# Interleaving the first two token tiles, full-row layout matmuls, and output tiles grouped by four in a fused attention and gMLP kernel

## The chip, the cores and the metric

The kernel runs on one core of a Trainium2 chip. The metric is the device time of one execution in microseconds (us). Before the change it is 211.75 us, the median of three runs (211.04 to 211.99).

The core has engines with queues of their own: TensorE (PE for its matmuls, PEld for its weight loads), VectorE (DVE), ScalarE (ACT), GpSimd (POOL) and SyncE (SP). Each works its queue in order and waits on semaphores. SP, ACT and POOL can issue DMA transfers, all of which run on the core's 16 DMA engines.

## The reference

The input x has 2048 tokens of 512 numbers (bf16). Two branches read it, and a gate mixes them:

```python
x = A_x
g = _sigmoid((x * gate_w).sum(-1, keepdims=True))
a = _A_ref(x, A_wqkv, A_w_phi, A_wo)
b = _B_ref(x, B_w_in, B_w_sp, B_b_sp, B_w_out)
return g * a + (1 - g) * b
```

Branch A is linear attention with 32 heads of 16. q and k are taken through a 16x16 matrix per head, and softmax(p) and softmax(-p), joined, are the features of each. The sums over tokens of features times v (kv) and of features (z) give num = phi_q kv and den = phi_q z; num / den goes through wo. Branch B is a gated MLP: z = gelu(x w_in) is cut into z1 and z2 of 688 columns; z2 is normalized per token, mixed over the tokens by w_sp (2048x2048), given a bias per token, multiplied with z1 and taken through w_out.

## The kernel before, in words

Tokens are worked in 16 tiles of 128. The tile framework allocates buffers from pools and sets the semaphores; a buffer that is used again waits for its earlier readers. On PE and ACT the order of the work is the program's own (`manual_schedule`); on the other engines the framework's scheduler orders instructions.

**Front** (lines 100 to 301). Identity, masks and constants are made on VectorE and POOL. SP loads the first token tiles (`xs`), part of the z2 weights (`w_z2`, one load for each 128 of 512 input rows) and later everything else; ACT issues three of the `w_z2` loads and `wphiE`. Tokens must lie transposed (`xT`) to be a matmul's weights. Tiles 0 to 3 are transposed on PE by `x_T` (four transposes, one VectorE copy), the others by DMA. `warm_up` matmuls on constants fill PE at the start (lines 277 to 284). `z2_tile` then multiplies a tile with `w_z2`: eight matmuls of 344 or 345 columns into one two-bank PSUM tile `zp`, then a Gelu on ACT and the statistics on VectorE. The extra column is the gate, put into `w_z2` by `gate_T` (line 237), which turns the loaded gate row by a transpose with 4 active rows. `b_T` (line 243) turns the bias with 16 active rows, and `wphi_fold` (line 248) spreads the 16x16 matrices with 16 active rows. Tile 0 and tile 1 follow one another, and `gate_T`, `x_T(1)`, `x_T(2)` and `x_T(3)` are put between their matmuls.

**k and v** (lines 496 to 519). For each tile: `k_tile` (four matmuls, two Exp, row sums, evening out on VectorE and POOL), `v_tile`, `kv_acc` into `kvacc`, and one half of a mixing tile, `gg_half`: 16 matmuls of 344 columns, one VectorE instruction into `ucat`, and after the second half a DMA transpose into `uT` from SP. Six q tiles (`q_tile`) are put into this stage too. A q tile's features are transposed by DMA into `eqT`.

**Attention and output** (lines 520 to 532). The slot i holds `attn_tile(i)` (eight matmuls of 68 columns into `at`, then `rden` and `o` on VectorE and a DMA transpose into `oT` from SP), `q_tile(i+6)` while there are any, one half of a mixing tile, and on even slots from 2 on `ba_pair`. `ba_pair` computes two output tiles: for each, four matmuls with `oT` and five with `uT` (`ba_main`), then one matmul for the 48 rows left over (`ba_rem`). In a pair these two matmuls have 64 active rows each, one in the upper and one in the lower half of the array. The results go out through ACT (`ba_store`: scale into `ob`, then a DMA issue on ACT's queue). Tiles 14 and 15 come last (`ba_tile`), tile 15 in two halves of 256 columns, the second of which goes through VectorE and SP.

[...] In the last two stages `kvacc`/`at` takes two, and the other six are the buffers of `mm` (`mm_tile`), which q, k, v, mixing and output tiles all take in turn. `ob` has the two buffers that are the default of its pool `work`.

Of the kernel before, what the change touches and what calls it, by code (L numbers as in the profile page):

```python
# [10 lines left out]
FP32 = mybir.dt.float32  # L11
# [3 lines left out]
P = 128  # L15
# [20 lines left out]
def kernel(  # L36
# [33 lines left out]
    z2all = pers.tile([P, NT, FH], BF16, name="z2all")  # L70
    z1all = pers.tile([P, NT, FH], BF16, name="z1all")
    wqkT = early.tile([P, 8, D], BF16, name="wqkT")
    wphiE = early.tile([DH, H, DH], BF16, name="wphiE")
    eexp = early.tile([DH, P], BF16, name="eexp")
    wphi = early.tile([P, NDT, P], BF16, name="wphi")
    mask_bd = early.tile([P, P], BF16, name="mask_bd")
    mask64 = pers.tile([P, NG, DH], BF16, name="mask64")
# [15 lines left out]

    ident = early.tile([P, P], BF16, name="ident")
    xs = early.tile([P, 4, D], BF16, name="xs")
    gaterow = early.tile([NDT, P], BF16, name="gaterow")
    brow = early.tile([NT, P], BF16, name="brow")
    zeros = early.tile([P, 32], BF16, name="zeros")

    w_in_v = B_w_in.rearrange("(dt p) f -> p dt f", p=P)  # L100

    ones32 = early.tile([P, 32], BF16, name="ones32")
    ramp = early.tile([P, 2, 32], BF16, name="ramp")
    nc.vector.memset(zeros[:], 0.0)
    nc.vector.memset(ones32[:], 1.0)
    nc.vector.tensor_tensor_scan(
# [5 lines left out]
    for q in range(4):  # L112
        qs = slice(32 * q, 32 * q + 32)
        nc.vector.tensor_tensor(
            out=ident[qs, qs], in0=ramp[qs, 0, :], in1=ramp[qs, 1, :], op=ALU.is_equal)
    nc.gpsimd.dma_start(out=gaterow[:, :], in_=gate_w.rearrange("(dt p) -> dt p", p=P))
    nc.gpsimd.dma_start(out=brow[:, :], in_=B_b_sp.rearrange("(t p) -> t p", p=P))
    def load_z2w(eng, dt):
        eng.dma_start(out=w_z2[:, dt, 0:FH], in_=w_in_v[:, dt, FH:F])

    nc.sync.dma_start(out=xs[:, 0, :], in_=x2[0:P, :])
    load_z2w(nc.scalar, 0)
    load_z2w(nc.sync, 1)
    load_z2w(nc.scalar, 2)
    nc.sync.dma_start(out=xs[:, 1, :], in_=x2[P:2 * P, :])
    load_z2w(nc.scalar, 3)
    nc.sync.dma_start(
        out=xs[:, 2:4, :], in_=x2[2 * P:4 * P, :].rearrange("(i p) d -> p i d", p=P))
# [7 lines left out]
            out=xT[:, :, q * CH:(q + 1) * CH], in_=x2[q * CH:(q + 1) * CH, :]  # L136
        )
    nc.sync.dma_start_transpose(out=wqkT[:, :, :], in_=A_wqkv[:, 0:2 * D])
    nc.scalar.dma_start(out=wphiE[:, :, :], in_=A_w_phi.rearrange("h e f -> e h f"))
    nc.sync.dma_start(  # L140
        out=wv_sb[:, :, :],
        in_=A_wqkv[:, 2 * D:3 * D].rearrange("(dt p) n -> p dt n", p=P),
# [37 lines left out]
    def z_mm(tt, wt, w, order=None, mid={}):  # L180
        zp = psA.tile([P, 2, CH], FP32, name="zp")
        for dt, j in order or [(dt, j) for dt in range(NDT) for j in range(2)]:
            n = HF if j == 0 else w - HF
            nc.tensor.matmul(  # L184
                zp[:, j, 0:n], lhsT=xT[:, dt, tt * P:(tt + 1) * P],
                rhs=wt[:, dt, j * HF:j * HF + n],
                start=(dt == 0), stop=(dt == NDT - 1),
            )
            for f in mid.get((dt, j), ()):
                f()  # L190
        return zp

    def z2_tile(tt, **kw):
        zp = z_mm(tt, w_z2, FH + 1, **kw)
# [5 lines left out]
        nc.vector.bn_aggr(out=mv[:, tt, :], in_=bn6[:, tt, :, :].rearrange("p j s -> p (j s)"))  # L200

    def z1_tile(tt):
        zp = z_mm(tt, w_z1, FH)
# [15 lines left out]
                op0=ALU.subtract, op1=ALU.mult,  # L219
            )  # L220

    wp = psA.tile([P, 2, CH], FP32, name="zp")

    def warm_up(n, w=CH):
        for _ in range(n):
# [4 lines left out]
    def x_T(i):  # L230
        tp = psF.tile([P, NDT, P], BF16, name="tp", tag="pq", bufs=2)
        for dt in range(NDT):
            nc.tensor.transpose(tp[:, dt, :], xs[:, i, dt * P:(dt + 1) * P], ident[:, :])  # L233
        with tc.high_priority():
            nc.vector.tensor_copy(out=xT[:, :, i * P:(i + 1) * P], in_=tp[:, :, :])  # L235

    def gate_T():
        gt = psF.tile([P, NDT], BF16, name="gt", tag="pq", bufs=2)
        nc.tensor.transpose(gt[:, :], gaterow[:, :], ident[0:NDT, 0:NDT])
        for dt in range(NDT):  # L240
            nc.vector.tensor_copy(out=w_z2[:, dt, FH:FH + 1], in_=gt[:, dt:dt + 1])

    def b_T():
        bt = psF.tile([P, NT], BF16, name="bt", tag="pq", bufs=2)
        nc.tensor.transpose(bt[:, :], brow[:, :], ident[0:NT, 0:NT])
        nc.vector.tensor_copy(out=bT[:, :], in_=bt[:, :])

    def wphi_fold():
# [26 lines left out]

    with tc.manual_schedule(engines={mybir.EngineType.PE, mybir.EngineType.Activation}):
        warm_up(7)
        x_T(0)
        warm_up(5, P)
        z2_tile(  # L280
            0, order=[(0, 0), (1, 0), (2, 0), (0, 1), (1, 1), (2, 1), (3, 0), (3, 1)],
            mid={(2, 0): [gate_T, lambda: x_T(1)], (2, 1): [lambda: warm_up(4, P)]},
        )
        z2_tile(1, mid={(1, 1): [lambda: x_T(2)], (2, 1): [lambda: x_T(3)]})
        z2_tile(2)
        z2_tile(3)
        b_T()
        for c in range(NCH):
            ts = list(range(c * 4, c * 4 + 4))
            for tt in ts:  # L290
                if c > 0:
                    z2_tile(tt)
                if c >= 2 and tt % 2 == 0:
                    fold(3 - c, (tt % 4) // 2)
            for tt in ts:
# [9 lines left out]
    early_cm.__exit__(None, None, None)  # L305
    psM = ctx.enter_context(
        tc.tile_pool(name="psM", bufs=1, space=bass.MemoryType.PSUM, reuse_waits="tile"))
    work = ctx.enter_context(tc.tile_pool(name="work", bufs=2, reuse_waits="tile"))
    kvp_cm = tc.tile_pool(name="kvp", bufs=2, side="right", reuse_waits="tile")
    kvp = kvp_cm.__enter__()  # L310

    def mm_tile():
        return psM.tile([P, CH], FP32, name="mm", tag="mm", bufs=6)

    def expo(pool, name, bufs, tt, w):
        ps = mm_tile()
# [103 lines left out]
    def attn_tile(tt):  # L420
        at = psM.tile([P, 8, P], FP32, name="at", tag="kvat", bufs=1)
        for g in range(8):
            nc.tensor.matmul(  # L423
                at[:, g, 0:AW], lhsT=eqTs[tt][:, g, :], rhs=kvz[:, g, :], start=True, stop=True)
# [12 lines left out]
        oTs[tt] = oT  # L437

    def u_T(tt):
        uT = work.tile([P, NFT, P], BF16, name="uT", bufs=9)  # L440
        nc.sync.dma_start_transpose(out=uT[:, :, :], in_=ucat[tt % NU][:, :])
        return uT

# [19 lines left out]
            nc.scalar.activation(out=ob[:, :], in_=acc, func=AF.Copy, scale=g_inv[:, tt:tt + 1])  # L463
            nc.scalar.dma_start(out=dst, in_=ob[:, :])

    def ba_tile(tt, nsplit=1):
        w = D // nsplit
        for h in range(nsplit):
            acc = mm_tile()
            ba_main(acc[:, 0:w], tt, h * w, (h + 1) * w)  # L470
            ba_rem(acc[:, 0:w], tt, slice(0, P), h * w, (h + 1) * w)
            ba_store(acc[:, 0:w], tt, h * w, (h + 1) * w, h > 0)

    def ba_pair(p):
        accs = [mm_tile() for _ in range(2)]
        for s_ in range(2):
            ba_main(accs[s_][:, :], 2 * p + s_)
        for s_ in range(2):
            ba_rem(accs[s_][:, :], 2 * p + s_, halves[s_])
        for s_ in range(2):  # L480
            ba_store(accs[s_][:, :], 2 * p + s_, 0, D, False)

    oTs = {}
    uTs = {}
    eqTs = {}
    Q_AT = (5, 7, 9, 11, 13, 15)
    ggs = [(tt, j) for tt in range(NT) for j in range(2)]

# [6 lines left out]
    with tc.manual_schedule(engines={mybir.EngineType.PE, mybir.EngineType.Activation}):  # L495
# [36 lines left out]
        ba_tile(15, nsplit=2)  # L532


# [28 lines left out]
```

## Time and profile before

| | |
|---|---|
| median of three runs | 211.75 us (211.04 to 211.99) |
| profiled execution | 211.67 us |
| its span, first to last instruction | 210.0 us |
| granted TensorE clock | 1.000 |
| start of the k stage on PE, by the chain of waits | 46.65 us |
| end of the last mixing tile's matmuls | 201.30 us |

A line of a timeline or of the chain of waits has the start, the length, the engine, the source line, what is written and what is read (buffer numbers left out), and how many instructions are merged. Times on PE are between the starts of pipelined matmuls: the mean length of one in the groups (309 ns for 344 columns) is longer than the 146 ns from one start to the next, and the latter is what each costs. "Idle before <- releaser" says how long the engine stood and what ended it. The `LNNN` in the lines are those of the kernel before.

### The profile page before, as it was taken

What the parts mean: (1) busy time and instruction counts of PE and PEld (TensorE: products, weight loads), DVE (VectorE), ACT (ScalarE), POOL (GpSimd) and SP (SyncE); (2) the same over time, 40 slices, a digit from 0 to 9 for tenths busy, and PEclk for the clock granted to TensorE, in tenths of its full rate; (3) what the DMA queues carried; (4) which work ended last, traced back from release to release, by engine and by line L of the source; (5) the groups of instructions that cost most, each with busy time, mean ns of one, the idle gap of its engine ahead of it and who ended that gap; (6) DMA issues with size and microseconds to landing.
All of it is one profiled execution on the core that took longest, in us unless ns stands there. A gap on an engine that the chain in (4) does not pass through costs nothing.

```text
span 210.0 us, 3753 instructions
## 1 busy us (share of the span) xinstructions
PE 203.5 (97%) x1437; PEld 121.8 (58%) x1456; DVE 131.6 (63%) x284; ACT 73.2 (35%) x119; POOL 46.4 (22%) x77
## 2 busy tenths in 40 slices
PE   8999999999999999999999999999999999999983
PEld 3666666665656565655556666464655555646442
DVE  3576786765996787979779669446554735415120
ACT  2366656668223323232332223150504240202120
POOL 7020202020643242425252223204040402000000
PEclk9999999999999999999999999999999999999999
DMA  6999999999910204214040599895567574435241
GB/s 196 263 164 242 256 274 189 267 274 185 272 37 3 39 4 85 54 36 89 3 87 0 118 333 146 162 128 112 125 92 150 104 134 83 107 64 101 41 112 50
DMA packets 88994, 27.20 MB, mean 130 GB/s; under 512 B 82864, under 2 KB 88976, under 8 KB 88976
## 3 DMA queue, kind: packets, MB, share of 16 engines
q1 hardware_dynamic: 83680, 22.45, 57.0%
q10 hardware_dynamic: 5232, 4.51, 7.0%
q8 instruction: 11, 0.18, 0.4%
q14 instruction: 7, 0.06, 0.1%
q0 software_dynamic: 64, 0.01, 0.0%
HBM read 4.41 MB, written 2.10 MB: 31 GB/s over the span
## 4 chain that ended last, share of the span: by engine, by line
PE 93%; DMA 3%; issue 1%; DVE 1%; SPq 0%
PE mm L410 36%; PE zp L184 18%; PE mm L318 13%; PE mm L449 8%; PE mm L358 7%; PE mm L447 6%; PE at L423 2%; DMA xs<-in_A_x_dram 2%; PE kvacc L374 2%; DMA uT<-ucat 1%; PE mm L452 1%; PE fps L265 1%; PE tp L233 0%; DVE ucat L415 0%; DVE ob L459 0%
## 5 line engine op out<-in xcount | busy, mean ns | idle before, releaser
L410 PE MATMUL mm<-z2all,wspT 128*128 128x344 bf16 x512 | 79.8, 309 | 0.1
L410 PEld LDWEIGHTS <-wspT 128*128 128x128 bf16 x512 | 48.7, 98 | 24.1
L184 PE MATMUL zp<-w_z,xT 128*128 128x344 bf16 (+1 forms) x256 | 39.9, 310 | 0.0
L184 PEld LDWEIGHTS <-xT 128*128 128x128 bf16 x256 | 24.3, 98 | 11.3 <-DVE xT L235 0.2
L322 ACT ACTIVATE eq<-mm 128x512 bf16<-128x512 f32 x32 | 17.4, 594 | 35.9 <-PE mm L318 23.4
L326 DVE TENSOR_REDUCE zs<-eq 128x64 f32<-128x1024 bf16 x16 | 19.4, 1216 | 15.5 <-ACT eq L322 15.5
L463 ACT ACTIVATE ob<-mm,g_inv 128x512 bf16<-128x512 f32 (+1 forms) x16 | 10.8, 674 | 51.6 <-PE mm L452 48.3
L335 POOL TENSOR_TENSOR eq<-eq,ratio 128x512 bf16<-128x512 bf16 x16 | 16.9, 1058 | 45.5 <-DVE ratio L334 24.0
L322 ACT ACTIVATE ek<-mm 128x512 bf16<-128x512 f32 x32 | 17.2, 602 | 25.0 <-PE mm L318 25.0
L415 DVE SCALAR_TENSOR_TENSOR ucat<-mm,bT,z1all 128x344 bf16<-128x344 f32 x32 | 18.0, 563 | 8.3 <-PE mm L410 7.4
L326 DVE TENSOR_REDUCE zs<-ek 128x64 f32<-128x1024 bf16 x16 | 19.2, 1208 | 2.8 <-ACT ek L322 2.8
L449 PE MATMUL mm<-slabs,uT 128*128 128x512 bf16 (+1 forms) x82 | 19.9, 366 | 0.9 <-DMA uT<-ucat 0.8
L426 DVE RECIPROCAL rden<-at 128x32 f32<-128x32 f32 x16 | 5.4, 338 | 22.6 <-PE at L423 22.6
L318 PEld LDWEIGHTS <-xT 128*128 128x128 bf16 x128 | 11.8, 97 | 10.8 <-issue 0.2
L335 POOL TENSOR_TENSOR ek<-ek,ratio 128x512 bf16<-128x512 bf16 x16 | 16.9, 1059 | 2.2 <-DVE ratio L334 1.3
L358 PE MATMUL mm<-wv_sb,xT 128*128 128x512 bf16 x63 | 16.4, 379 | 0.1
L318 PE MATMUL mm<-wk_p,xT 128*128 128x512 bf16 x57 | 15.8, 379 | 0.4
L447 PE MATMUL mm<-slabs,oT 128*128 128x512 bf16 (+1 forms) x65 | 16.0, 366 | 0.2
L318 PE MATMUL mm<-wq_p,xT 128*128 128x512 bf16 x59 | 15.6, 378 | 0.2
L196 ACT ACTIVATE z2all<-zp 128x688 bf16<-128x688 f32 x16 | 11.9, 744 | 10.8 <-PE zp L184 10.8
L199 DVE BATCH_NORM_STATS2 bn<-z2all 128x6 f32<-128x344 bf16 x32 | 14.9, 502 | 0.0
L204 ACT ACTIVATE z1all<-zp 128x688 bf16<-128x688 f32 x16 | 11.9, 744 | 6.9 <-PE zp L184 6.9
(73 smaller groups left out, 151.9 us busy)
## 6 DMA issues: line engine op xcount, KB each, us to landing
out_dram<-ob ACTq DMA_DIRECT2D x15, 128.0 KB, 2.6
slabs<-in_B_w_out_dram ACTq DMA_DIRECT2D x2, 640.0 KB, 6.8
w_z<-in_B_w_in_dram SPq DMA_DIRECT2D x2, 344.0 KB, 4.6
w_z<-in_B_w_in_dram ACTq DMA_DIRECT2D x3, 172.0 KB, 3.5
wv_sb<-in_A_wqkv_dram SPq DMA_DIRECT2D x1, 512.0 KB, 4.5
slabs<-in_A_wo_dram ACTq DMA_DIRECT2D x1, 512.0 KB, 3.6
xs<-in_A_x_dram SPq DMA_DIRECT2D x2, 128.0 KB, 3.6
xs<-in_A_x_dram SPq DMA_DIRECT2D x1, 256.0 KB, 5.0
```

The lines of the kernel that those rows point to most:

```text
L184: nc.tensor.matmul(zp[:, j, 0:n], lhsT=xT[:, dt, tt * P:(tt + 1) * P], rhs=wt[:, dt, j * HF:j * HF + n], start=(dt == 0), stop=(dt == NDT ...
L196: nc.scalar.activation(out=z2v, in_=zp[:, :, 0:HF], func=AF.Gelu_apprx_tanh)
L199: nc.vector.bn_stats(out=bn6[:, tt, j, :], in_=z2v[:, j, :])
L318: nc.tensor.matmul(ps[:, :], lhsT=xT[:, dt, tt * P:(tt + 1) * P], rhs=w[:, dt, :], start=(dt == 0), stop=(dt == NDT - 1))
L322: nc.scalar.activation(out=e[:, :, a, :], in_=ps[:, :].rearrange("p (h f) -> p h f", f=DH), func=AF.Exp, scale=1.0 - 2.0 * a)
L326: nc.vector.tensor_reduce(out=z[:].rearrange("p h a -> p (h a)"), in_=e[:].rearrange("p h a f -> p (h a) f"), axis=AX.X, op=ALU.add,)
L335: nc.gpsimd.tensor_tensor(out=e[:, :, 1, :], in0=e[:, :, 1, :], in1=ratio[:, :, None].to_broadcast([P, H, DH]), op=ALU.mult)
L358: nc.tensor.matmul(v_ps[:, :], lhsT=xT[:, dt, tt * P:(tt + 1) * P], rhs=wv_sb[:, dt, :], start=(dt == 0), stop=(dt == NDT - 1))
L410: nc.tensor.matmul(gp[:, 0:HF], lhsT=wspT[:, st, tt * P:(tt + 1) * P], rhs=z2all[:, st, j * HF:(j + 1) * HF], start=(st == 0), stop=(st == ...
L415: nc.vector.scalar_tensor_tensor(out=ucat[tt % NU][:, c0 + j * HF:c0 + (j + 1) * HF], in0=gp[:, 0:HF], scalar=bT[:, tt:tt + 1], in1=z1all[ ...
L447: nc.tensor.matmul(acc, lhsT=oT[:, g, :], rhs=wo_t[:, g, c0:c1], start=(g == 0), stop=False)
L449: nc.tensor.matmul(acc, lhsT=uT[:, i + ft, :], rhs=w_main[i][:, ft, c0:c1], start=False, stop=False)
```

## The change

- Front: tile 0 and tile 1 have a function of their own, `z2_first_two`, which interleaves their matmuls in a new order with two short warm-ups instead of nine. `x_T(0)` is split: the first 128 columns are copied by VectorE, the other 384 by ACT. The second token tile's load goes ahead of a weight load on SP, and weight loads 1 and 2 swap queues.
- `gate_T`, `b_T` and `wphi_fold` work on 128 rows: their row inputs become 128-row tiles whose other rows are set to zero by memsets on VectorE and POOL. `gate_T` and `b_T` become matmuls with the identity.
- Output: `ba_step` computes one output tile's main part in each slot into one of four accumulators of their own. After the last tile of a group of four (in the end, of two) the left-over rows of the whole group and then its stores follow. The other PSUM tiles of this stage have two buffers.
- `attn_tile` runs one slot ahead, behind the mixing half; slot 0 has two mixing halves, and the last mixing half moves one slot earlier.
- Tile 15 is cut at column 384 instead of 256. `eqT` has 7 buffers instead of 8, `oT` 5 instead of 4, `uT` 11 instead of 9.

```diff
-    wphiE = early.tile([DH, H, DH], BF16, name="wphiE")
-    eexp = early.tile([DH, P], BF16, name="eexp")
+    wphiE = early.tile([P, H, DH], BF16, name="wphiE")
+    eexp = early.tile([P, P], BF16, name="eexp")
-    gaterow = early.tile([NDT, P], BF16, name="gaterow")
-    brow = early.tile([NT, P], BF16, name="brow")
+    gaterow = early.tile([P, P], BF16, name="gaterow")
+    brow = early.tile([P, P], BF16, name="brow")
+    nc.vector.memset(gaterow[:], 0.0)
-    nc.gpsimd.dma_start(out=gaterow[:, :], in_=gate_w.rearrange("(dt p) -> dt p", p=P))
-    nc.gpsimd.dma_start(out=brow[:, :], in_=B_b_sp.rearrange("(t p) -> t p", p=P))
+    nc.gpsimd.dma_start(out=gaterow[0:NDT, :], in_=gate_w.rearrange("(dt p) -> dt p", p=P))
+    nc.gpsimd.memset(brow[:], 0.0)
+    nc.gpsimd.memset(wphiE[:], 0.0)
+    nc.gpsimd.dma_start(out=brow[0:NT, :], in_=B_b_sp.rearrange("(t p) -> t p", p=P))
     nc.sync.dma_start(out=xs[:, 0, :], in_=x2[0:P, :])
     load_z2w(nc.scalar, 0)
-    load_z2w(nc.sync, 1)
-    load_z2w(nc.scalar, 2)
     nc.sync.dma_start(out=xs[:, 1, :], in_=x2[P:2 * P, :])
+    load_z2w(nc.scalar, 1)
+    load_z2w(nc.sync, 2)
     load_z2w(nc.scalar, 3)
-    nc.scalar.dma_start(out=wphiE[:, :, :], in_=A_w_phi.rearrange("h e f -> e h f"))
+    nc.scalar.dma_start(out=wphiE[0:DH, :, :], in_=A_w_phi.rearrange("h e f -> e h f"))
...
+    def z2_first_two():
+        zps = [zp_tile() for _ in range(2)]
+
+        def one(tt, dt, j):
+            z_one(zps[tt], tt, w_z2, FH + 1, dt, j)
+
+        x_T(0, True)
+        warm_up(2, P)
+        one(0, 0, 0)
+        x_T(1)
+        one(0, 1, 0)
+        one(1, 0, 0)
+        one(1, 1, 0)
+        gate_T()
+        one(0, 2, 0)
+        one(1, 2, 0)
+        for dt in range(3):
+            one(0, dt, 1)
+        x_T(2)
+        one(0, 3, 0)
+        one(0, 3, 1)
+        z2_out(0, zps[0])
+        for dt in range(3):
+            one(1, dt, 1)
+        x_T(3)
+        one(1, 3, 0)
+        one(1, 3, 1)
+        z2_out(1, zps[1])
...
+    def x_T(i, split=False):
+        for k, dts in enumerate([range(1), range(1, NDT)] if split else [range(NDT)]):
+            tp = psF.tile([P, NDT, P], BF16, name="tp", tag="pq", bufs=2)
+            for dt in dts:
+                nc.tensor.transpose(tp[:, dt, :], xs[:, i, dt * P:(dt + 1) * P], ident[:, :])
+            d = slice(dts[0], dts[-1] + 1)
+            if k == 1:
+                nc.scalar.copy(out=xT[:, d, i * P:(i + 1) * P], in_=tp[:, d, :])
+            else:
+                with tc.high_priority():
+                    nc.vector.tensor_copy(out=xT[:, d, i * P:(i + 1) * P], in_=tp[:, d, :])
     def gate_T():
-        nc.tensor.transpose(gt[:, :], gaterow[:, :], ident[0:NDT, 0:NDT])
-        for dt in range(NDT):
-            nc.vector.tensor_copy(out=w_z2[:, dt, FH:FH + 1], in_=gt[:, dt:dt + 1])
+        nc.tensor.matmul(gt[:, :], lhsT=gaterow[:, :], rhs=ident[:, 0:NDT], start=True, stop=True)
+        nc.vector.tensor_copy(out=w_z2[:, :, FH], in_=gt[:, :])
     def b_T():
-        nc.tensor.transpose(bt[:, :], brow[:, :], ident[0:NT, 0:NT])
+        nc.tensor.matmul(bt[:, :], lhsT=brow[:, :], rhs=ident[:, 0:NT], start=True, stop=True)
...
     with tc.manual_schedule(engines={mybir.EngineType.PE, mybir.EngineType.Activation}):
         warm_up(7)
-        x_T(0)
-        warm_up(5, P)
-        z2_tile(
-            0, order=[(0, 0), (1, 0), (2, 0), (0, 1), (1, 1), (2, 1), (3, 0), (3, 1)],
-            mid={(2, 0): [gate_T, lambda: x_T(1)], (2, 1): [lambda: warm_up(4, P)]},
-        )
-        z2_tile(1, mid={(1, 1): [lambda: x_T(2)], (2, 1): [lambda: x_T(3)]})
+        z2_first_two()
...
+    psK_cm = tc.tile_pool(name="psK", bufs=6, space=bass.MemoryType.PSUM, reuse_waits="tile")
+    mm_pool = psK_cm.__enter__()
     def mm_tile():
-        return psM.tile([P, CH], FP32, name="mm", tag="mm", bufs=6)
+        return mm_pool.tile([P, CH], FP32, name="mm")
-        eqT = work.tile([P, 8, P], BF16, name="eqT", bufs=8)
+        eqT = work.tile([P, 8, P], BF16, name="eqT", bufs=7)
-        oT = work.tile([P, NG, P], BF16, name="oT", bufs=4)
+        oT = work.tile([P, NG, P], BF16, name="oT", bufs=5)
-        uT = work.tile([P, NFT, P], BF16, name="uT", bufs=9)
+        uT = work.tile([P, NFT, P], BF16, name="uT", bufs=11)
...
+    def acc_tile():
+        return psC.tile([P, CH], FP32, name="acc")
+    def ba_step(tt):
+        group = next(g for g in BA_GROUPS if tt in g)
+        accs[tt] = acc_tile()
+        ba_main(accs[tt][:, :], tt)
+        if tt == group[-1]:
+            for t in group:
+                ba_rem(accs[t][:, :], t, halves[t % 2])
+            for t in group:
+                ba_store(accs[t][:, :], t, 0, D, False)
+    BA_GROUPS = [range(0, 4), range(4, 8), range(8, 12), range(12, 14)]
...
-        for i in range(NT):
-            attn_tile(i)
+        psK_cm.__exit__(None, None, None)
+        mm_pool = ctx.enter_context(
+            tc.tile_pool(name="psG", bufs=2, space=bass.MemoryType.PSUM, reuse_waits="tile"))
+        psC = ctx.enter_context(
+            tc.tile_pool(name="psC", bufs=4, space=bass.MemoryType.PSUM, reuse_waits="tile"))
+        attn_tile(0)
+        for i in range(NT - 1):
             if i + nq < NT:
                 q_tile(i + nq)
-            if ggs:
+            gg_next()
+            attn_tile(i + 1)
+            if i == 0:
                 gg_next()
-            if i >= 2 and i % 2 == 0:
-                ba_pair((i - 2) // 2)
+            elif i < NT - 1:
+                ba_step(i - 1)
         ba_tile(14)
-        ba_tile(15, nsplit=2)
+        ba_tile(15, cuts=(0, 384, D))
```

More of the change, by code (lines that the diff above doesn't have):

```diff
@@ L178, with zp_tile, z_one, z_mm @@
     psA = psA_cm.__enter__()
[L180 to L187, printed above, removed]
-            )
-            for f in mid.get((dt, j), ()):
-                f()
-        return zp
-    def z2_tile(tt, **kw):
-        zp = z_mm(tt, w_z2, FH + 1, **kw)
+    def zp_tile():
+        return psA.tile([P, 2, CH], FP32, name="zp")
+    def z_one(zp, tt, wt, w, dt, j):
+        n = HF if j == 0 else w - HF
+        nc.tensor.matmul(
+            zp[:, j, 0:n], lhsT=xT[:, dt, tt * P:(tt + 1) * P],
+            rhs=wt[:, dt, j * HF:j * HF + n],
+            start=(dt == 0), stop=(dt == NDT - 1),
+        )
+    def z_mm(tt, wt, w):
+        zp = zp_tile()
+        for dt in range(NDT):
+            for j in range(2):
+                z_one(zp, tt, wt, w, dt, j)
+        return zp
+    def z2_out(tt, zp):
         z2v = z2all[:, tt, :].rearrange("p (j n) -> p j n", j=2)
@@ L200, in z2_tile @@
         nc.vector.bn_aggr(out=mv[:, tt, :], in_=bn6[:, tt, :, :].rearrange("p j s -> p (j s)"))
+    def z2_tile(tt):
+        z2_out(tt, z_mm(tt, w_z2, FH + 1))
+    def z2_first_two():
[24 more added lines that the diff above has]
+        z2_out(1, zps[1])
     def z1_tile(tt):
@@ L220, in z2_norm @@
             )
-    wp = psA.tile([P, 2, CH], FP32, name="zp")
+    wp = zp_tile()
     def warm_up(n, w=CH):
@@ L228, in warm_up @@
                 rhs=nc.const_aps.tensor(1.0, [P, w], BF16), start=True, stop=True)
-    def x_T(i):
-        tp = psF.tile([P, NDT, P], BF16, name="tp", tag="pq", bufs=2)
-        for dt in range(NDT):
-            nc.tensor.transpose(tp[:, dt, :], xs[:, i, dt * P:(dt + 1) * P], ident[:, :])
-        with tc.high_priority():
-            nc.vector.tensor_copy(out=xT[:, :, i * P:(i + 1) * P], in_=tp[:, :, :])
+    def x_T(i, split=False):
[9 more added lines that the diff above has]
+                    nc.vector.tensor_copy(out=xT[:, d, i * P:(i + 1) * P], in_=tp[:, d, :])
     def gate_T():
-        gt = psF.tile([P, NDT], BF16, name="gt", tag="pq", bufs=2)
-        nc.tensor.transpose(gt[:, :], gaterow[:, :], ident[0:NDT, 0:NDT])
-        for dt in range(NDT):
-            nc.vector.tensor_copy(out=w_z2[:, dt, FH:FH + 1], in_=gt[:, dt:dt + 1])
+        gt = psF.tile([P, NDT], FP32, name="gt", tag="pq", bufs=2)
+        nc.tensor.matmul(gt[:, :], lhsT=gaterow[:, :], rhs=ident[:, 0:NDT], start=True, stop=True)
+        nc.vector.tensor_copy(out=w_z2[:, :, FH], in_=gt[:, :])
     def b_T():
-        bt = psF.tile([P, NT], BF16, name="bt", tag="pq", bufs=2)
-        nc.tensor.transpose(bt[:, :], brow[:, :], ident[0:NT, 0:NT])
+        bt = psF.tile([P, NT], FP32, name="bt", tag="pq", bufs=2)
+        nc.tensor.matmul(bt[:, :], lhsT=brow[:, :], rhs=ident[:, 0:NT], start=True, stop=True)
         nc.vector.tensor_copy(out=bT[:, :], in_=bt[:, :])
@@ L277 @@
         warm_up(7)
-        x_T(0)
-        warm_up(5, P)
-        z2_tile(
-            0, order=[(0, 0), (1, 0), (2, 0), (0, 1), (1, 1), (2, 1), (3, 0), (3, 1)],
-            mid={(2, 0): [gate_T, lambda: x_T(1)], (2, 1): [lambda: warm_up(4, P)]},
-        )
-        z2_tile(1, mid={(1, 1): [lambda: x_T(2)], (2, 1): [lambda: x_T(3)]})
+        z2_first_two()
         z2_tile(2)
@@ L464, in ba_store, with ba_tile @@
             nc.scalar.dma_start(out=dst, in_=ob[:, :])
[L466 to L481, printed above, removed]
+    def acc_tile():
+        return psC.tile([P, CH], FP32, name="acc")
+    def ba_tile(tt, cuts=(0, D)):
+        for h, (c0, c1) in enumerate(zip(cuts, cuts[1:])):
+            acc = acc_tile()[:, 0:c1 - c0]
+            ba_main(acc, tt, c0, c1)
+            ba_rem(acc, tt, slice(0, P), c0, c1)
+            ba_store(acc, tt, c0, c1, h > 0)
+    def ba_step(tt):
[7 more added lines that the diff above has]
+                ba_store(accs[t][:, :], t, 0, D, False)
     oTs = {}
@@ L485 @@
     eqTs = {}
+    accs = {}
+    BA_GROUPS = [range(0, 4), range(4, 8), range(8, 12), range(12, 14)]
     Q_AT = (5, 7, 9, 11, 13, 15)
```

## The prediction

> **What bounds the kernel now.** I read the page's engine shares first, then PE's waits, then the chain of waits stage by stage, then ScalarE's timeline, because the change rearranges what ScalarE and PE share. The shares:
>
> ```profile
> PE 203.5 (97%) x1437; PEld 121.8 (58%) x1456; DVE 131.6 (63%) x284; ACT 73.2 (35%) x119; POOL 46.4 (22%) x77
> ```
>
> PE is busy through the span and the others are not. What PE waits for, by the waits of PE:
>
> ```profile
> PE zp L226 <- PEq L547: 0.8, 1, 0.8
> PE mm L449 <- DMA uT<-ucat: 0.8, 1, 0.8
> PE tp L233 <- DMA xs<-in_A_x_dram: 0.5, 1, 0.5
> ```
>
> Only 2.1 us. So this change cannot win by removing large waits; it can win at the start, at the end, and in what the "busy" share hides: warm-ups and drains. Everything on PE is on the path, so a microsecond saved or lost there is one of span.
>
> **The front.** The chain of waits from 4 to 13 us (start, length, what):
>
> ```profile
> 1.74 4.41 DMA xs<-in_A_x_dram
> 6.19 0.40 PE tp L233 x4
> ...
> 8.88 2.63 PE zp L184 x18
> 11.51 0.11 PE bt L245
> ```
>
> PE stands until the second token tile lands at 6.15, its load being third on SP's queue (issued 1.74). A matmul of 344 columns takes 2.63/18 = 0.146. Tile 2 starts two matmuls into the x18 piece (PE's timeline puts its first start at 8.71): at 9.01. In the changed order: warm-ups end at 3.79 as now; x_T(0) at 0.107 a transpose (half speed) to 4.22; two warm-ups to 4.43. Now the 512-column VectorE copy starts 0.24 after its last transpose and takes 0.42; the 128-column piece, 0.2 by estimate, ends under the warm-ups. One matmul (0.29 at half speed) to 4.72. xs1 is now second on SP, where w_z2[1] landed at 4.53 with more bytes, so x_T(1) runs to 5.1. Its copy ends at 5.75; two matmuls of tile 1 to 6.05. w_z2[2], third on SP, takes the place that landed at 6.15: 6.2, then five matmuls to 6.93. x_T(2) needs xs2-3, which landed at 7.19 (issued 2.21, 5.0 to land). If that stays, 7.24 + 0.22 + seven matmuls 1.02 + x_T(3) 0.22 = 8.70: gain 0.3. If it lands by 6.93: 8.39, gain 0.6. I take 0.45. For earlier speaks that wphiE (16 KB in small pieces, 5.2 to land in the DMA view) now waits on POOL for its memset (128x512, 0.53 by the slabs memset) and comes later on the same DMA engines. Bounds -0.3 to 0.8: the same memset holds ScalarE's queue at the wphiE issue (2.23 now), with the table load (1.28) and the second part of x_T(0)'s copy (128x384, 0.58 between the 0.475 of 256 and the 0.687 of 512 columns) behind it. That copy then ends near 5.3, and its matmul still comes before 5.75, while PE waits for x_T(1)'s copy. VectorE's gaterow memset (0.11, as ident's) is over long before xs0. If ScalarE were another 0.5 later, the gain would be gone.
>
> [...] The trace shows seven warm-ups of 427 ns and short ones of 107, then 147 ns per 344 columns from 5.15 on. The change drops seven of nine short warm-ups. [...] By the row PE is continuously busy in my layout from 0.85 to 5.25[...]. I take 0.
>
> **128-row layout matmuls.** The chain from 24 to 32:
>
> ```profile
> 25.74 0.32 PE wps L251 x4
> ...
> 27.34 0.22 PE fps L265 x4
> ```
>
> Four 128-column matmuls with 16 rows cost 0.10 more than four with 128; the eight after them take 1.28 instead of 1.17. So 0.2 goes. b_T takes 0.11 plus the entry gap (11.34 to 11.44) and would cost about 0.06 with 128 rows: 0.15. gate_T lay in the xs1 wait: 0. The single copy of its column replaces four of 0.15 on VectorE, off the path. Sum 0.35.
>
> **Left-over rows by fours.** The chain from 129 to 165:
>
> ```profile
> 146.51 0.32 PE mm L452 x2
> 146.83 0.36 PE at L423 x8
> 147.19 0.86 PE mm L318 x4
> 148.06 2.33 PE mm L410 x16
> 150.39 0.26 PE at L423 x8
> ```
>
> Two 64-row matmuls of 512 columns run beside each other in 0.32, 0.10 more than one full matmul (0.86/4 = 0.215); the eight matmuls after them take 0.36 instead of 0.26. So entering and leaving the half-row shape costs 0.20. Seven pairs become three fours and one pair: 3 x 0.20 = 0.6. If four did not overlap as two by two, 0.215 more each, and the gain is nil; the pair is the nearest row, so 0.6.
>
> **The end.** The chain from 196 to 210:
>
> ```profile
> 201.93 2.76 DMA uT<-ucat
> ...
> 204.73 0.72 PE mm L449 x5
> ...
> 206.69 0.48 DVE ob L459
> ```
>
> PE's timeline has the last oT matmul before the wait begin its 0.108 at 203.69; the next starts at 204.73: 0.94 lost. In the changed order the last gg is followed by attn (0.26), ba_step(13) (9 x 0.215 = 1.94), a pair (0.32) and ba_tile(14) (2.15): 4.7 until tile 15 is wanted. uT(15) lands 0.61 + 0.04 + 2.76 = 3.4 after gg. oT(15), issued behind it on SP (1.21), lands at 1.87 + 2.5 = 4.4, or 4.97 with the 3.1 of a lone transpose, bounding its wait at 0.3. I take 0: gain 0.94. The last store is 128 columns, not 256: VectorE 0.48 to about 0.33 (344 columns of ucat take 0.57), 0.15. Together 1.1.
>
> Gains: 0.45 + 0.35 + 0.6 + 1.1 = 2.5.
>
> **What it adds: a burst on ScalarE.** The timeline of ScalarE (ACT) around one pair:
>
> ```profile
> 146.87 0.69 ACT L463 ACTIVATE ob<-mm,g_inv 128x512 bf16<-128x512 f32 x1 [5.40 <-PE mm L452]
> 147.59 0.34 ACTq L464 DMA_DIRECT2D out_dram<-ob  x1
> 148.03 0.69 ACT L463 ACTIVATE ob<-mm,g_inv 128x512 bf16<-128x512 f32 x1 [0.47 <-ACT ob L463]
> 148.74 0.36 ACTq L464 DMA_DIRECT2D out_dram<-ob  x1
> 149.20 1.09 ACT L322 ACTIVATE eq<-mm 128x512 bf16<-128x512 f32 x2 [0.49 <-ACT ob L463]
> ```
>
> A store takes 1.16 of ScalarE, and the next q tile's two Exp queue behind the stores in program order. Now that harms nobody: mm has six buffers. Afterwards four stores stand ahead of the Exp, ob has two buffers, so the third waits for the first to land, and q and gg share two PSUM buffers: q(12) cannot start until q(11)'s Exp are over.
>
> Let q(11) start at 0, just after the four's left-over rows. Store 1 is active from -0.11 (0.36 after its matmul, as above), its DMA leaves at 0.61; store 2's at 1.77. The landing times of single stores in the ob view are 2.0 and 2.2 where a transpose went just before, 1.7 with none, 2.6 behind oT's. At 2.1 store 3 starts at 2.78, store 4 at 3.94 (store 2 has then just landed), the Exp at 5.10, ending 6.19. PE wants the buffer after 0.86 + 2.33 + 0.26 + 1.94 = 5.39. So PE stands 0.86. This happens after tiles 0-3 (q(12)) and 4-7 (the gg after q(15)); after 8-11 no Exp is left. Sum 1.7. Bounds: 0.5 each at 1.7, 1.4 each at 2.6. [...] Here all four go through ScalarE. By the pair's row alone (two stores, 1.16 each) the Exp would end at about 3.3 and nothing would wait[...].
>
> VectorE's queue behind a late Exp: q(11)'s row sums (1.2), then whatever is ordered after them. If the gg's ucat (0.57), ready at 3.2, stood behind, the next gg would wait 0.9 more; I take 0, its order following readiness. The two gg at slot 0 meet VectorE's backlog: 0 to 0.6, taken 0. SP's late eqT is wanted only four slots later. The attention step moves behind gg: its VectorE work and its oT issue on SP now come after ucat and uT, and oT(i+1), 3.1 to land, is wanted two slots (over 9 us) later: 0. POOL's brow load goes behind two memsets (0.7) and is wanted near 11: 0. eqT with seven, oT with five, uT with eleven buffers each free a slot before need: 0. The end's stores have two ob buffers for tiles 12, 13, 14, ready 2.5 apart: 0.
>
> Net: -2.5 + 1.7 = -0.8 against the profiled execution's 211.67 (span 210.0 and 1.67 around it), 210.9; it lies 0.08 under the median of the runs, so I leave it.
>
> **Rivals.** (a) No hold: stores land faster or queue differently, so PE never waits. Then 211.7 - 2.5 = 209.2. For it: 1.7 was seen; against it: two ob buffers and four stores need over 5.39. (b) The front does not change, because xs2-3 and w_z2[2] set it: 211.3 to 211.7 with the hold. That edit then does not do what it says. (c) Slower: out stores land at 4.1 and 3.7, as the ob view has for the first pair (136 to 141), next to two transposes. Store 3 then waits till 4.8, the Exp end at 8.2, PE stands 2.8 twice: 211.7 - 2.5 + 5.6 = 214.8. It turns slower when a hold exceeds 1.25, a landing of about 2.5, and beyond 0.5% at 3.0. Against it: one pair of seven did so.
>
> **How the numbers follow.** A difference under 0.5% (1.06 us) can hardly be told from none. The hold case, 0.60: 209.8 to 211.9, half below 210.7. Case (a), 0.17: 208.9 to 209.7. Case (b), 0.11. Case (c), 0.09 beyond 0.5%; VectorE's order, 0.03, near 211.8. Faster 0.30 + 0.17 = 0.47; same 0.30 + 0.11 + 0.03 = 0.44; slower 0.09. Range 209.2 to 212.2.
>
> **What would show it.** A PE gap of about 0.9 before the matmuls of q(12) and before the gg after q(15), ended by ACT eq; store 3 of each four starting on its DMA's landing; wps at 0.22; left-over rows 0.53 for four; no uT wait at the end; tile 2 at about 8.55. Wrong if PE shows no wait for ACT in the attention slots, or a half-clock stretch after 5.3.

## The result and the profile after

The changed kernel takes 210.24 us (median of four runs, 210.04 to 210.44) against 211.62 us for the kernel before on the same chip. The ratio is 0.9937, with a 95% interval of 0.9912 to 0.9962: 0.6% faster, 1.4 us. The profiled execution took 210.28 us with a span of 208.6, so the two spans differ by 1.39. All line numbers from here on are those of the kernel that a block names.

The waits of PE in the changed kernel (engine, tile, line, releaser: us in total, times, longest):

```profile
PE zp L265 <- PEq L598: 0.8, 1, 0.8
PE mm L449 <- DVE ucat L454: 0.4, 1, 0.4
PE zp L188 <- DMA w_z<-in_B_w_in_dram: 0.3, 1, 0.3
PE zp L188 <- DVE xT L279: 0.2, 1, 0.2
```

The wait for uT is gone. A wait for a weight load and one for VectorE's `ucat` are new. Now the same stages as before the change. The front, by the chain of waits:

```profile
1.76 5.12 DMA w_z<-in_B_w_in_dram
6.88 0.04 issue
6.92 0.89 PE zp L188 x5
...
8.99 2.63 PE zp L188 x18
11.62 0.01 PE bt L288
```

PE no longer stands for the second token tile but for weight load 2, which landed at 6.88. Tile 2 starts two matmuls into the x18 piece; in PE's timeline that is 9.12, against 9.01 before. The bias matmul, 0.11 before, is 0.01. The head matrices, chain from 24 to 32:

```profile
25.66 0.22 PE wps L294 x4
25.88 1.17 PE zp L188 x8
27.05 0.22 PE fps L308 x4
```

The four `wps` matmuls now take what the four `fps` take (0.22, with 0.32 before), and the eight behind them are at 1.17 where they had 1.28. In the attention slots, by the chain from 190 to 209, a four of left-over rows and what follows, then the end:

```profile
190.99 0.54 PE acc L491 x4
191.53 2.44 PE mm L449 x16
...
203.07 0.22 PE acc L491
203.28 0.65 PE acc L486 x4
...
205.51 0.35 DVE ob L498
```

Four left-over rows take 0.54, and the sixteen matmuls after them 2.44 instead of 2.33: one entry and one exit for four tiles. At the end PE runs through, and the last store takes 0.35 on VectorE instead of 0.48.

The predicted burst is there too. The chain from 148 to 157:

```profile
149.20 0.69 ACT ob L502
...
149.91 2.44 DMA out_dram<-ob
...
152.43 0.70 ACT ob L502
...
153.59 0.69 ACT ob L502
...
154.75 1.09 ACT eq L361 x2
155.84 0.04 issue
155.88 1.18 PE mm L449 x7
```

Store 3 starts on the landing of store 1, store 4 follows, the two Exp of q(11) come last. Yet what waits for them is not q(12) but the mixing half behind it (L449), and it waits only 0.31 (0.529 between two starts in PE's timeline where 0.215 is usual). PE's waits above do not list so short a stand. The second burst, whose first store took 4.0 to land, holds nobody: the mixing half after q(15) starts before the Exp of q(15), by the timelines of PE and ScalarE:

```profile
177.24 2.50 PE L449 MATMUL mm<-z2all,wspT 128*128 128x344 bf16 x16
178.82 1.08 ACT L361 ACTIVATE eq<-mm 128x512 bf16<-128x512 f32 x2 [0.47 <-ACT ob L502]
```

The other new wait is in slot 0, chain from 123 to 128:

```profile
122.93 1.18 PE mm L449 x8
124.11 0.03 issue
124.13 0.59 DVE ucat L454
124.72 0.04 issue
124.76 2.49 PE mm L449 x16
```

The second mixing half of slot 0 stands behind VectorE's `ucat` of the first, which begins as soon as that half's matmuls are done: 0.58 between the starts (0.609 less 0.03). Only the eight attention matmuls lie in between.

By stage, from PE's starts in the two profiles: first matmul of tile 4 at 11.55 before and 11.49 after (-0.06); first attention matmul at 120.90 and 120.48 (another -0.35); from there to the last matmul 85.48 and 84.77 (-0.71); from that to the end of the span 3.58 and 3.32 (-0.26).

### The profile page after: what moved, and what is told of

Read it like the earlier page. It is cut to its first block, busy times and chain, and to the rows that moved or that the text cites. A ratio compares the mean times of both kernels' runs of the same rounds, so it can differ in the third digit from the quotient of the medians.

```text
span 208.6 us, 3745 instructions
## 1 busy us (share of the span) xinstructions
PE 202.5 (97%) x1432; PEld 121.5 (58%) x1449; DVE 131.2 (63%) x282; ACT 75.0 (36%) x121; POOL 47.0 (23%) x79
## 4 chain that ended last, share of the span: by engine, by line
PE 91%; DMA 4%; ACT 2%; issue 1%; DVE 0%; SPq 0%; ACTq 0%
PE mm L449 35%; PE zp L188 18%; PE mm L357 12%; PE acc L488 8%; PE mm L397 7%; PE acc L486 6%; DMA w_z<-in_B_w_in_dram 2%; PE kvacc L413 2%; PE at L462 2%; DMA out_dram<-ob 1%; PE acc L491 1%; ACT ob L502 1%; PE fps L308 1%; ACT eq L361 1%; ACTq L503 0%
## 5 line engine op out<-in xcount | busy, mean ns | idle before, releaser
L449 PE MATMUL mm<-z2all,wspT 128*128 128x344 bf16 x512 | 79.9, 309 | 0.6 <-DVE ucat L454 0.4
L449 PEld LDWEIGHTS <-wspT 128*128 128x128 bf16 x512 | 49.0, 98 | 26.3 <-issue 1.4
L188 PEld LDWEIGHTS <-xT 128*128 128x128 bf16 x256 | 24.5, 98 | 12.1 <-DVE xT L279 0.7
L454 DVE SCALAR_TENSOR_TENSOR ucat<-mm,bT,z1all 128x344 bf16<-128x344 f32 x32 | 17.4, 545 | 21.2 <-PE mm L449 21.2
L502 ACT ACTIVATE ob<-acc,g_inv 128x512 bf16<-128x512 f32 (+1 forms) x16 | 10.9, 680 | 33.9 <-PE acc L491 23.2
L488 PE MATMUL acc<-slabs,uT 128*128 128x512 bf16 (+2 forms) x85 | 20.1, 366 | 0.0
L357 PEld LDWEIGHTS <-xT 128*128 128x128 bf16 x128 | 12.3, 98 | 13.0 <-PE acc L491 0.8
L357 PE MATMUL mm<-wq_p,xT 128*128 128x512 bf16 x62 | 16.3, 379 | 0.1
L486 PE MATMUL acc<-slabs,oT 128*128 128x512 bf16 (+2 forms) x61 | 15.6, 365 | 0.4
L488 PEld LDWEIGHTS <-uT 128*128 128x128 bf16 x85 | 8.2, 98 | 9.2
```

The costliest lines, as they stand in the source:

```text
L188: nc.tensor.matmul(zp[:, j, 0:n], lhsT=xT[:, dt, tt * P:(tt + 1) * P], rhs=wt[:, dt, j * HF:j * HF + n], start=(dt == 0), stop=(dt == NDT ...
L357: nc.tensor.matmul(ps[:, :], lhsT=xT[:, dt, tt * P:(tt + 1) * P], rhs=w[:, dt, :], start=(dt == 0), stop=(dt == NDT - 1))
L449: nc.tensor.matmul(gp[:, 0:HF], lhsT=wspT[:, st, tt * P:(tt + 1) * P], rhs=z2all[:, st, j * HF:(j + 1) * HF], start=(st == 0), stop=(st == ...
L454: nc.vector.scalar_tensor_tensor(out=ucat[tt % NU][:, c0 + j * HF:c0 + (j + 1) * HF], in0=gp[:, 0:HF], scalar=bT[:, tt:tt + 1], in1=z1all[ ...
L486: nc.tensor.matmul(acc, lhsT=oT[:, g, :], rhs=wo_t[:, g, c0:c1], start=(g == 0), stop=False)
L488: nc.tensor.matmul(acc, lhsT=uT[:, i + ft, :], rhs=w_main[i][:, ft, c0:c1], start=False, stop=False)
```

## The experiments

Theory: the gains of the prediction came about except at the front. The hold did not, because the two PSUM buffers of q and mixing tiles are not taken in turn, as the prediction's sum needed. In the program as built q(12) has the buffer of the mixing half before it, not q(11)'s, and the half after q(15) has the other one, not q(15)'s. Slot 0's second half has the buffer of the half just before it, which makes the 0.58. The rival: the burst was never in the way, whoever has which buffer.

**Strict turn.** Edit to the changed kernel, for the tiles of the attention slots only:

```diff
-        return mm_pool.tile([P, CH], FP32, name="mm")
+        if slots is None:
+            return mm_pool.tile([P, CH], FP32, name="mm")
+        return mm_pool.tile([P, CH], FP32, name="mm", tag=f"g{slots.pop(0)}", bufs=1)
...
+        slots = [0, 1] * 13
         attn_tile(0)
```

> The changed kernel with the two PSUM buffers of q and mixing tiles taken strictly in turn. My theory: the prediction took a strict turn for granted, and the allocator didn't take one: it gave q(12) the buffer of the mixing half before it, and the half after q(15) the other one too. With a strict turn the predicted holds should appear: PE stands about 1.2 us before q(12) and again before the mixing half after q(15) (0.3 and none in the changed kernel), while the 0.58 at the second mixing half of slot 0 goes: net +1.5, 211.7 us. Rival: the store burst never was in the way, whoever has the buffers; then only the 0.58 goes, 209.7.

Measured: 215.48 us (214.42 to 215.71), ratio to the kernel before 1.0165 (1.014 to 1.019). Both holds are there, by the waits of PE (first two rows), and the second by its chain:

```profile
PE mm L453 <- ACT eq L365: 2.9, 1, 2.9
PE mm L361 <- ACT eq L365: 1.1, 1, 1.1
```

```profile
173.35 4.37 DMA out_dram<-ob
...
177.81 0.70 ACT ob L506
...
178.97 0.70 ACT ob L506
...
181.26 3.89 PE mm L453 x16
```

The first is 1.26 between starts, as expected. The second is 3.1, not 1.2, because store 1 took 4.37 to land. In the changed kernel the same store took 4.0 (issued 172.43) and held nobody. The sixteen matmuls after the hold take 3.89 instead of 2.33. The windows of this kernel show the granted clock in them (each row: us, then busy time of each engine with its instructions, the granted clock, DMA):

```profile
core 0: us, PE busy (x) PEld busy (x) DVE busy (x) ACT busy (x) POOL busy (x), PEclk, DMA share, GB/s
173.90:177.30 3.40, 3.40 (x30) 2.12 (x28) 1.11 (x3) 0.58 (x1) 0.00 (x0) 1.00 1.13 141
177.31:180.72 3.41, 1.01 (x5) 0.38 (x4) 0.48 (x1) 1.97 (x4) 0.00 (x0) 1.00 0.48 129
180.72:184.13 3.41, 2.87 (x11) 1.52 (x11) 1.76 (x3) 0.49 (x2) 0.85 (x1) 0.50 0.07 21
184.13:187.54 3.41, 3.36 (x26) 1.97 (x26) 1.59 (x3) 0.00 (x0) 0.20 (x1) 1.00 0.58 109
```

Behind 3.41 us in which PE was busy for 1.01, the granted clock is 0.50 for 3.41 us, and the sixteen matmuls that begin at 181.26 take 1.56 more than without it. Four of the five runs have a granted clock of 0.992 over the span; the fifth, with 1.000, is the one of 214.42. In slot 0 the 0.58 went, but 0.73 came at the next half, which then took the buffer of the half before it. The total is 3.8 us above the 211.7 expected: the longer second hold, the half clock and these 0.73 make it. The rival falls, since both holds came with the turn.

**Strict turn with four store buffers.**

```diff
-        ob = work.tile([P, c1 - c0], BF16, name=f"ob{c1 - c0}")
+        ob = work.tile([P, c1 - c0], BF16, name=f"ob{c1 - c0}", bufs=4 if c1 - c0 == D else 1)
```

> The strict turn of the two PSUM buffers with four store buffers. If landings make most of the hold, the two holds of 1.26 and 3.1 us shrink to about 0.3 each (four stores at 1.16, two Exp, against 5.39 until the buffer is wanted)[...], and the time is 210.1 us. If ScalarE's own queue makes it, they stay near 1.2 and the time is above 212.

Measured: 210.32 us (209.87 to 211.25), ratio 0.9946 (0.9927 to 0.9965). The chain at q(12), whose four matmuls take 0.86 without a hold:

```profile
154.74 1.02 PE mm L361 x4
155.76 2.33 PE mm L453 x16
```

The second hold, before the half after q(15), is found in the same way. The holds are 0.16 and 0.25 instead of 1.26 and 3.1, and the half-clock stretch is gone (the granted clock is 1.000 over the span). So the landings made most of the holds, and ScalarE's own queue the 0.16 and 0.25 that are left.

**Four store buffers alone**, in the changed kernel.

> The changed kernel with four buffers for the 512-column store tile instead of two, so that stores 3 and 4 of a group don't wait for the landing of stores 1 and 2. If the landings make the hold, the Exp of q(11) end about 0.9 us earlier and the 0.31 us before the mixing half behind q(12) goes: 209.9 us. If ScalarE's own 1.16 us per store makes it, little changes: 210.2.

Measured: 209.70 us (209.36 to 210.32), ratio 0.9909 (0.9892 to 0.9927). The Exp of q(11) end 1.0 earlier after store 1, the 0.31 is gone, and from the first attention matmul to the last matmul it is 84.46 instead of 84.77. The rest of its lead in these two profiles, 0.24, lies ahead of that stage, in the front.

**Pairs instead of fours.**

```diff
-    BA_GROUPS = [range(0, 4), range(4, 8), range(8, 12), range(12, 14)]
+    BA_GROUPS = [range(t, t + 2) for t in range(0, 14, 2)]
```

> The changed kernel with its left-over rows and stores in pairs instead of fours. By the prediction's sum three more entries and exits of the half-row shape cost 0.20 us each, +0.6, and the hold of 0.31 goes: net +0.3, 210.5 us. Rival: the fours are worth nothing by themselves (their second pair costs as much as an entry), then 209.9.

Measured: 210.56 us (210.15 to 211.18), ratio 0.9950 (0.9932 to 0.9969). Its chain around a pair:

```profile
148.77 0.32 PE acc L491 x2
149.09 0.97 PE mm L357 x4
```

0.10 on entering and 0.11 on leaving, seven times again, and no wait for the Exp. From the first attention matmul to the last it takes 85.09, 0.32 more than the fours: +0.6 and -0.3, as expected. Beside the fours with four store buffers (84.46), which have no such hold either, it is 0.63 more, so the fours by themselves are worth the 0.6.

**The old front** in the changed kernel: `x_T(0)`, five and four short warm-ups, the old order of tiles 0 and 1 and of the first loads.

> The changed kernel with the old front: the order of tiles 0 and 1, nine short warm-ups and the old order of the first loads; the layout matmuls on 128 rows and everything behind stay. If the new front is worth nothing or less, as the two traces say (tile 2 starts at 9.12 us after, 9.01 before), this gives 210.1 to 210.3 us, tile 2 at about 9.0. If the new front does bring the 0.45 us of the prediction and only this one profile hid it, this gives about 210.7.

Measured: 210.09 us (209.92 to 210.69), ratio 0.9930 (0.9912 to 0.9948): not slower than the changed kernel, though the interval, about 0.4 us either way, leaves room for a few tenths. In its profile tile 2 starts at 9.22 and tile 4 at 11.59.

**The layout matmuls alone**, in the kernel before: `gaterow`, `brow`, `wphiE` and `eexp` on 128 rows with their memsets, `gate_T` and `b_T` as matmuls.

> The kernel before with nothing but the 128-row layout matmuls (gate, bias and head matrices, with their memsets). The prediction's sum gives 0.35 us: 0.15 at the bias, 0.2 at the head matrices, nothing at the gate: 211.3 us, and the first attention matmul 0.35 earlier than 120.90. Rival: the drains of the old shapes lay beside other waits, then nothing: 211.65.

Measured: 211.12 us beside 211.51 for the kernel before, ratio 0.9984 (0.9971 to 0.9997): 0.39 us by the medians, and 0.35 lies inside the interval. In its profile the first attention matmul is at 120.81, only 0.09 earlier, because tile 2 started 0.31 later than in the profile before (9.32); from there on it is 0.40 earlier.

**The head matrices' load later.**

```diff
-    nc.scalar.dma_start(out=wphiE[0:DH, :, :], in_=A_w_phi.rearrange("h e f -> e h f"))
+    nc.sync.dma_start(out=wphiE[0:DH, :, :], in_=A_w_phi.rearrange("h e f -> e h f"))
     nc.sync.dma_start_transpose(out=wqkT[:, :, :], in_=A_wqkv[:, 0:2 * D])
```

> The changed kernel with the load of the head matrices (512 pieces of 32 bytes) issued by SP just ahead of the q and k weights instead of by ACT among the first loads. If these pieces are what holds back the weight load that PE waits for at 6.5 to 6.9 us, loads 2 and 3 of z2's weights and tokens 256 to 511 land by about 6.0 and 6.7, tile 2 starts at about 8.5 instead of 9.1, and the time is 209.8 us. If the order of the large loads sets it, tile 2 stays at 8.9 to 9.1: 210.2.

Measured: 209.87 us (209.68 to 210.31), ratio 0.9926 (0.9911 to 0.9942). Its front:

```profile
1.76 4.50 DMA w_z<-in_B_w_in_dram
...
8.37 2.63 PE zp L188 x18
11.00 0.01 PE bt L288
```

Weight load 2 lands at 6.26 and tokens 256 to 511 at 6.81; everything behind is 0.62 earlier than in the first profile of the changed kernel. But that profile was the odd one: in the six others with the changed front as it is, weight load 2 lands at 5.60 to 6.25 without this edit. Over all seven the tokens land at 7.10 to 7.70 and tile 4 starts at 11.00 to 11.59 (mean 11.27). With the later load the tokens land at 6.81, 6.88 and 7.36 and tile 4 starts at 10.87, 10.78 and 11.26, beside one execution told below. That fits a gain of about 0.3 through the tokens, not through weight load 2. The times do not secure it: of three pairs of kernels that differ in this load alone, this one is 0.3 faster, one (below) the same and one 0.2 slower.

**Buffers by hand with four store buffers**, and the same **with the later load**. Here `slots = [0, 1, 0, 1, 0, 1, 0, 1, 0, 1, 0, 1, 0] + [0, 1] * 4 + [1, 0, 1, 0, 1]`.

> The changed kernel with four store buffers, and with the two PSUM buffers dealt out by hand: the second mixing half of slot 0 gets the buffer of q(6), q(12) that of the mixing half before it, the mixing half after q(15) the other one than q(15)'s. If the allocator's choice is what spared and what cost the time, no wait of PE on the Exp is left, and the 0.58 us of slot 0 go or shrink to VectorE's backlog of about 0.1: 209.1 to 209.3 us. Rival: the wait only moves to the next mixing half, 209.7.

> Both of the last two edits together, as a version that may beat both kernels: if each gives what it should, 208.8 us; if the head matrices' load does not matter, the same as the kernel with the hand-dealt buffers alone.

Measured: 209.93 us (209.57 to 210.35), ratio 0.9927 (0.9909 to 0.9944), and 210.08 us (209.44 to 210.95), ratio 0.9936 (0.9913 to 0.9959). No wait for an Exp is left, but 0.73 before the half in slot 1 took the place of the 0.58: the rival was right. VectorE works q(6)'s row sums (1.2) ahead of the second half's `ucat`. The second version's profile has the shorter span, 207.7 against 208.5, but its times are no better; whether the later load helps there stays open.

**Four store buffers and the later load, buffers left to the allocator.**

> The changed kernel with four store buffers and the later load of the head matrices, the PSUM buffers left to the allocator. By the two runs that did one of these each: 0.31 and about 0.4 under the changed kernel, 209.5 us, the 0.58 of slot 0 still there.

Measured: 209.69 us (209.13 to 212.22 in 13 runs), ratio 0.9908 (0.9880 to 0.9935). That is the ratio of four store buffers alone (0.9909), so the later load brought nothing here, and the 209.5 was missed. The profiled execution was the 212.22. Its windows (columns as above):

```profile
4.30:7.71 3.41, 1.78 (x15) 0.83 (x13) 0.61 (x3) 1.76 (x2) 0.76 (x6) 1.00 0.97 307
7.72:11.12 3.40, 3.40 (x18) 2.13 (x17) 0.62 (x3) 0.74 (x1) 0.00 (x0) 0.50 1.51 179
```

Its later first loads all landed late. PE stood 1.4 for the gate row, which landed at 7.32; but weight load 2, which PE needs next, came only at 7.12, and tokens 256 to 511 at 8.34. Then the granted clock was 0.50 from 7.72 to 11.12, and tile 4 started at 13.69, 2.4 later than the mean of the seven. What made the loads late, and what the old front would have paid, was not tried.

**A version that beats both.** Four store buffers, the later load, and the extra mixing half moved from slot 0 to slot 1, ahead of its output tile, with `slots = [0, 1, 0, 1, 0] + [1, 0] * 4 + [0, 1] * 4 + [1, 0, 1, 0, 1]`:

```diff
-            if i == 0:
+            if i == 1:
                 gg_next()
-            elif i < NT - 1:
+            if 0 < i < NT - 1:
                 ba_step(i - 1)
```

> A version that may beat both kernels: the changed kernel with four store buffers, the head matrices' load later, and the second mixing half of slot 0 moved to slot 1, ahead of its output tile, with the PSUM buffers dealt out by hand so that no half follows on a buffer whose reader has hardly begun. If the 0.58 us of slot 0 come only from that half standing right behind the one whose buffer it takes, they go, and with 0.31 of the hold and about 0.45 at the front the time is about 208.9 us. Rival: VectorE's backlog at that place moves the wait to the next user again, 209.5.

Measured: 208.99 us (208.46 to 209.50), ratio 0.9873 (0.9853 to 0.9893). PE's waits are down to two:

```profile
PE zp L265 <- PEq L603: 0.8, 1, 0.8
PE zp L188 <- DVE xT L279: 0.3, 1, 0.3
```

From the first attention matmul to the last it takes 83.91, 0.86 less than the changed kernel: the 0.58 and the 0.31.

**The changed kernel again.**

> The changed kernel once more, for the spread of its front: in its first profile tile 4 started at 11.5 us, in the others with the same front between 11.0 and 11.6. Expected 210.2 us again, tile 4 anywhere in that range, with the same waits of 0.58 and 0.31 behind it.

Measured: 210.39 us (209.82 to 210.98), ratio 0.9942 (0.9920 to 0.9963). Tile 4 starts at 11.19, and the 0.58 is there again; the 0.31 is 0.21 here. The first output tile waits 0.3 for oT(0): PE reaches that tile earlier than before the change, so a landing with little margin can show (0.3 here, 0.1 in the strict turn, none in the first profile). The prediction had no term for that.

## Why the prediction was right in sign and short in size

It said 210.9 with a range of 209.2 to 212.2; the profiled execution took 210.28 and the median is 210.24. The change is faster, by 0.6%, just over the half percent of the outcome given 0.47. The terms, predicted and measured in the first profile:

| step | predicted | measured |
|---|---|---|
| front up to tile 2 | -0.45 | +0.11 (about -0.3 over seven profiles) |
| layout matmuls | -0.35 | -0.39 (bias 0.18, head matrices 0.21) |
| left-over rows by fours | -0.6 | -0.6 |
| the end | -1.1 | -0.94 wait, -0.26 behind the last matmul, -0.07 not assigned |
| hold of the store burst | +1.7 | +0.31 |
| slot 0, second mixing half | 0 (0 to 0.6) | +0.58 |
| not in the sum: entry of the k stage | | -0.13 |
| sum | -0.8 | -1.4 |

That the sum came so near is in part luck: the hold that hardly came (1.4 less) paid for the front (0.6 short) and for slot 0 (0.6 more). The time fell into the band of the hold case (209.8 to 211.9) without that hold. Of the two signs that the prediction gave for being wrong the first all but showed (PE's waits name no ACT in the attention slots, and only the chain has the 0.31), and the second did: in the first profile the full clock is on record from 6.12 only, past 5.3, and the four transposes of `x_T(1)` at 4.99 took 0.107 each, those of `x_T(2)` at 7.65 0.055.

**Right as worked out.** The entry and exit of a reduced-row shape cost 0.10 each here, as predicted; the pairs (0.10 and 0.11) and the layout by itself (`wps` at 0.22 instead of 0.32, the eight matmuls behind it at 1.17 instead of 1.28) bear this out. uT(15) and oT(15) landed before their use. The burst's own arithmetic held: store 1 at -0.11 of q(11)'s start (149.19 against 149.30), store 3 on a landing, the Exp ending at 6.5 where 6.19 was worked out from landings of 2.1 that were 2.4. The one pair of seven before with landings of about 4 was no outlier: the second burst saw 4.0 and 4.37. Rival (c) therefore had its landing right for one burst of two, and the strict turn shows its price: 3.1 and the half clock.

**Wrong: "q and gg share two PSUM buffers: q(12) cannot start until q(11)'s Exp are over".** Two buffers in a pool were read as a ring. The allocator did not deal them in turn, so q(12) passed the burst and the mixing half behind it had 0.86 more time. The strict turn shows that the path was right for a ring, but the size too small: 1.26 and 3.1, and 1.6 of half clock, where the sum had 0.86 twice. This one assumption decided the sign: 215.5 against 210.2.

**Wrong: "wphiE ... now waits on POOL for its memset".** POOL's timeline in the changed kernel:

```profile
0.80 0.20 POOL L118 MEMSET brow<- 128x128 bf16 x1 [0.29 <-POOLq L598]
0.95 0.53 POOL L119 MEMSET wphiE<- 128x512 bf16 x1
1.42 0.77 POOL L117 DMA_DIRECT2D gaterow<-in_gate_w_dram  x1
```

The scheduler put the memsets ahead of the gate row's load, POOL stood idle there anyway, and wphiE left at 2.21 as before. So the reason given for earlier tokens fell away. In the first profile the first tokens landed at 4.04 instead of 3.62 and weight load 2 at 6.88 where 6.15 was assumed, which the six other profiles do not repeat (5.60 to 6.25). The tokens 256 to 511 landed at 7.10 to 7.70 over the seven, 7.19 before: no earlier. On average tile 2 starts at 9.18 in the three profiles with the old front and at 8.91 in the seven with the new one. That is the prediction's lower case, 0.3; the timed run with the old front shows none of it.

**Right to charge nothing for the dropped warm-ups.** The 0 was an estimate from the trace before; what brings the full clock was not shown. In the clock records of the profiles it begins at 5.10 (before the change), 5.99 and 3.59 us in the three with the old front and at 3.90 to 6.80 in the eleven with the new one. It varies by 2.4 us among the three and by 2.9 among the eleven, so three and eleven profiles show no difference. In the first profile the late full clock (6.12) cost nothing: from 5.42 to 6.14 PE worked one matmul and then stood for VectorE's copy of `xT`.

**Slot 0: inside the bounds, for another reason.** The prediction thought of VectorE's backlog. In the changed kernel VectorE had been idle for 1.71 us when the first half's `ucat` came. PE waited because the second half has the same buffer: the ring again, which would have given it the other one. With a strict turn VectorE's backlog does show, as the 0.73 one half later, behind q(6)'s row sums. The timeline before had it: the `ucat` of slot 1's mixing half came 1.1 us after its matmuls (127.8 to 128.90), behind two row sums.

## What to carry to other kernels

Before a wait for a reused buffer is priced, look up which buffer the built program gives each tile: a pool is not a ring, and here that decided between 210.2 and 215.5 us. If an engine issues several stores in a row and something else queues behind them, give the stores as many buffers as the row is long; the landing of a store (1.7 to 4.4 us here) is otherwise part of the engine's queue (in the strict turn 215.48 us with two buffers, 210.32 with four). A hold on PE can be dearer than its length: behind the 3.1 here the granted clock was 0.50 for 3.41 us, which cost 1.6 more; behind the 1.26 the next sixteen matmuls took 2.50 (at 156.80), as the sixteen ahead of it had (at 150.14).

## What the runs showed of the hardware that was not expected

- The granted clock was 0.50 for 3.41 us in the strict turn and for 3.40 in the execution with the late first loads; in the 3.41 us ahead PE was busy for 1.01 and 1.78. At the end of the kernel it went to 0.50 at 209.90 before the change and at 207.51 in the changed kernel; in the 3.4 us ahead PE was busy for 0.17 and 1.37. What decides when it falls was not shown.
- In all twelve profiles with the changed output stage, whether in pairs or fours, one store lands late: the one issued at 171 to 174 us takes 4.0 to 4.4 (4.0 in the changed kernel, 4.37 in the strict turn) and the one behind it 3.6 to 3.9 (3.6 in the changed kernel), while most others take 1.7 to 2.7. In the kernel before, the pair issued at 136.4 and 137.5 took 4.1 and 3.7. What makes these late was not shown.
- In the changed kernel ScalarE loads two tables in the front, 1.28 us at 2.69 ahead of its first copy of `xT` and 1.28 at 5.23 ahead of the Gelu; in the kernel before it loads one there, 1.28 at 2.71, and its first activation is the Gelu. Both loads lay beside other work.
